# Attention rebuilt: float32 scores of two heads in the two row halves of the array, units of query chunks, a written-out order, 13 weight slots

## The chip, the cores and the metric

One core of one Trainium2 chip. The metric is device microseconds of one execution of the program. The engines go by their names in the profile: PE (TensorE, matrix products), DVE (VectorE), ACT (ScalarE), POOL (GpSimd) and SP (whose queue issues the DMAs).

## What is computed

Causal attention over 2 batches of 12 heads (448 tokens, head dimension 64), its output as 896 tokens by 768, then two feed-forward blocks. The reference, cut:

```python
scores = scale * np.matmul(q, k.transpose(0, 1, 3, 2))      # (2, 12, 448, 448), causal mask
attn = exp(scores - max) / sum
x = np.matmul(attn, v)                                      # -> (896, 768)
h = x @ w_in                                                # 768 x 2048
g = np.where(h >= 1, h, np.where(h <= -1, 0.0, (h + 1) ** 2 / 4))
x = g @ w_out                                               # 2048 x 768
xn = x / sqrt(mean(x * x) + 1e-6) * rms_g
x = (silu(xn @ w_gate) * (xn @ w_val)) @ w_out              # 768 x 1536 twice, 1536 x 768
```

## The kernel before

Activations are held transposed, features on the 128 partitions and 448 tokens (one batch, "half" h) along the free dimension. Every large product is a **three-pass product**: weight and activation are each split into a float32r high part and a low remainder, and three matmuls of 128x448 add up high·high, high·low and low·high. There are 576 such matmuls in the first product (w_in: 16 blocks m, two halves, 6 chunks of contraction), 576 in the second (w_out: 16 chunks kk, two halves), 864 in the gated product and 432 in the last one.

**Weights.** They arrive as 64-bit words, 68 blocks of 128x768. Each block goes through `w_scale` (POOL), `w_sign`, `w_high`, `w_low` (DVE), then `w_hi` (a cast, on POOL for the first blocks and on ACT for the others) and `w_lo` (a subtraction on POOL) into one of the slots; `w_low` also issues the load of the block after next. `w_pace(x)` puts x blocks' worth of these steps into the program at the place where it is called, `w_cap` says how far it may go, and `RATE` holds the values of x. The first MRET = 9 of 13 slots hold w_in blocks while attention runs; the other four are taken up by the split q and k.

**Attention.** One step s of the loop handles one head: `scores` (per head: four bf16 matmuls that write the causal mask into the banks, then eight float32r matmuls, since q and k are split into high and low parts by `split_q` and `split_k` on DVE and POOL; the first pair of heads is `plain`: float32, with the other head's rows of q at zero), `softmax` (per chunk of 112 queries a maximum on DVE and an exponential with its sum on ACT), `transposes` of the head before (ten on PE) and `evac` (three copies on ACT). Once for each pair of heads: `factor` (1/sum: two small DVE operations, a POOL operation, four transposes and a copy on ACT), `pv` (the product with v, both heads at once in the two column halves) and `xsplit` (a DVE product and two POOL operations). Seven PSUM banks go round in one ring for scores, transposes and factor. In the second batch the first 8 blocks of the first product for the first half are laid between as `fill`, in parts of three matmuls, in two banks; `moe_act` finishes each block.

**Order.** Attention is ordered by the Tile scheduler: program order is not the order on the engines there. From the rest of the first product on, `manual_schedule` keeps the written order. Each engine runs its queue strictly in order.

## Time and profile before

| | |
|---|---|
| three runs | 667.75, 669.01, 672.34 us (median 669.01) |
| profiled execution, span | 669.7 us |
| attention (last product with v issued) | 0 to 165.3 us |
| rest of the first product | 165.3 to 257.1 us |
| second product | 257.1 to 405.7 us |
| gated product, from its 37th matmul | 405.7 to 576.8 us |
| last product | 576.8 to 666.1 us |

The span runs from the first to the last instruction of the profiled execution. Busy times of PE include the drain of each matmul, so a busy PE can still take more work.

### The profile page before, as it was taken

The page shows a single profiled execution, that of the slowest core. Times are in us where ns is not written, and L with a number is a line of the kernel's source. Part 1 is how long each engine was busy: PE and PEld are TensorE (multiplying, and loading weights), DVE is VectorE, ACT ScalarE, POOL GpSimd, SP SyncE. Part 2 cuts the span into 40 slices and gives each one's busy share as a digit, 9 for nine tenths or more (in the row PEclk, how much of TensorE's full clock was granted, in tenths as well). Part 3 has the DMA queues.
Part 4 walks back from the last instruction along what each step waited for, and adds up shares of the span by engine and source line. Part 5 has one row for each costly group of instructions (what it writes and reads, how often), then busy time and mean ns, then how long its engine had stood idle before and what let it go on. Part 6 is the DMA issues. An engine that isn't in the chain of part 4 may idle for free.

```text
span 669.7 us, 8507 instructions
## 1 busy us (share of the span) xinstructions
PE 622.5 (93%) x3220; PEld 544.5 (81%) x3220; DVE 494.5 (74%) x634; ACT 211.5 (32%) x488; POOL 278.7 (42%) x215
## 2 busy tenths in 40 slices
PE   4898896899999997799999989999999999999997
PEld 3766674778999996688789978999999999999996
DVE  4999999954598889889544887998887776887100
ACT  2767642453222132222331243122222122422100
POOL 3477787662054343446300440444334434246200
PEclk9998988899999999899999999999999999999999
DMA  8445533220033333333200430324233223255000
GB/s 236 120 117 158 148 113 109 80 90 1 2 139 109 128 103 133 112 125 140 95 0 1 132 104 8 135 94 142 94 98 136 97 95 119 72 179 174 27 32 37
DMA packets 18377, 67.56 MB, mean 101 GB/s; under 512 B 2272, under 2 KB 8288, under 8 KB 18336
## 3 DMA queue, kind: packets, MB, share of 16 engines
q1 hardware_dynamic: 18336, 67.02, 31.3%
q8 instruction: 25, 0.41, 0.2%
q14 instruction: 16, 0.13, 0.1%
HBM read 64.26 MB, written 2.75 MB: 100 GB/s over the span
## 4 chain that ended last, share of the span: by engine, by line
PE 60%; DVE 30%; issue 3%; ACT 3%; DMA 2%; POOL 1%; SPq 0%; ACTq 0%; POOLq 0%; DVEq 0%
PE b L367 30%; PE b L662 13%; PE b L552 10%; DVE af L171 5%; DVE af L159 4%; DVE af L165 4%; DVE af L376 4%; DVE nm L305 3%; DVE ar L507 2%; PE b L351 2%; PE b L288 2%; PE b L334 2%; DVE ar L251 2%; DVE ar L252 2%; DVE ar L260 1%
## 5 line engine op out<-in xcount | busy, mean ns | idle before, releaser
L367 PE MATMUL b<-ar 128*128 128x448 f32 x1440 | 306.4, 371 | 0.0
L367 PEld LDWEIGHTS b<-ar 128*128 128x128 f32 x1440 | 270.1, 189 | 28.0 <-ACT af L341 0.7
L186 POOL TENSOR_TENSOR ar<-af,ar 128x768 fp32r<-128x768 f32 x68 | 127.9, 1881 | 197.2 <-ACT ar L178 196.7
L552 PE MATMUL b<-ar 128*128 128x448 f32 x576 | 124.3, 375 | 14.6 <-DVE ar L507 7.6
L552 PEld LDWEIGHTS b<-ar 128*128 128x128 f32 x576 | 109.7, 192 | 28.9 <-DVE ar L507 10.4
L178 ACT CAST ar<-af 128x768 fp32r<-128x768 f32 x59 | 49.4, 836 | 235.0 <-DVE af L171 235.0
L154 POOL TENSOR_SCALAR af<-af 128x768 f32<-128x768 f32 x68 | 75.2, 1106 | 96.7 <-DMA af<-in_w_out 44.4
L662 PE MATMUL b<-ar 128*128 128x448 f32 x432 | 89.4, 368 | 0.0
L662 PEld LDWEIGHTS b<-ar 128*128 128x128 f32 x432 | 81.1, 188 | 8.2
L171 DVE SCALAR_TENSOR_TENSOR af<-af 128x768 int32<-128x768 int32 x68 | 84.1, 1237 | 1.7
L165 DVE SCALAR_TENSOR_TENSOR af<-af 128x768 int32<-128x768 int32 x68 | 76.7, 1128 | 1.8
L159 DVE TENSOR_SCALAR af<-af 128x768 int32<-128x768 int32 x68 | 61.3, 902 | 12.8 <-POOL af L154 11.4
L309 ACT ACTIVATE af<-b,nm 112x448 f32<-112x448 f32 (+1 forms) x96 | 46.6, 504 | 63.2 <-DVE nm L305 63.0
L507 DVE TENSOR_TENSOR ar<-af,ar 128x448 fp32r<-128x448 f32 x32 | 32.6, 1024 | 27.1 <-ACT ar L506 26.9
L376 DVE SCALAR_TENSOR_TENSOR af<-af 128x448 f32<-128x448 f32 x32 | 32.5, 1016 | 23.4 <-ACT af L375 23.4
L334 PE MATMUL b<-ident,af 112*112 112x112 f32 x240 | 31.3, 277 | 17.1 <-ACT af L309 17.1
L334 PEld LDWEIGHTS b<-ident,af 112*112 112x112 f32 x240 | 26.8, 143 | 21.9 <-ACT af L309 16.0
L261 POOL TENSOR_TENSOR ar<-af,ar 128x448 fp32r<-128x448 f32 x22 | 31.2, 1419 | 23.0 <-DVE ar L260 17.7
L305 DVE TENSOR_REDUCE nm<-b 112x1 f32<-112x448 f32 (+1 forms) x96 | 37.1, 439 | 4.1 <-PE b L288 3.8
L288 PE MATMUL b<-ar 128*112 128x256 f32 (+2 forms) x176 | 35.4, 337 | 0.0
L628 DVE TENSOR_TENSOR af<-af 128x448 f32<-128x448 f32 x24 | 30.5, 1269 | 6.5 <-ACT af L626 5.1
L288 PEld LDWEIGHTS b<-ar 128*112 128x112 f32 x176 | 26.4, 183 | 8.2 <-issue 4.8
(59 smaller groups left out, 452.2 us busy)
## 6 DMA issues: line engine op xcount, KB each, us to landing
af<-in_w_out SPq DMA_DIRECT2D x28, 768.0 KB, 4.2
af<-in_w_in SPq DMA_DIRECT2D x16, 768.0 KB, 4.4
af<-in_w_gate SPq DMA_DIRECT2D x12, 768.0 KB, 4.2
af<-in_w_val SPq DMA_DIRECT2D x12, 768.0 KB, 4.2
af<-in_kT SPq DMA_DIRECT2D x23, 224.0 KB, 3.9
af<-in_v SPq DMA_DIRECT2D x12, 224.0 KB, 3.4
out_T<-af SPq DMA_DIRECT2D x12, 224.0 KB, 1.9
af<-in_qT SPq DMA_DIRECT2D x12, 112.0 KB, 2.4
```

The source lines that it names most:

```text
L154: nc.gpsimd.tensor_scalar(out=c, in0=c, scalar1=2.0 ** -112, scalar2=1.0, op0=ALU.mult, op1=ALU.mult)
L159: nc.vector.tensor_scalar(out=wt[n % 2].bitcast(I32), in0=words(n, 1, I32), scalar1=-2 ** 31, scalar2=0, op0=ALU.bitwise_and, op1=ALU.bitw ...
L165: nc.vector.scalar_tensor_tensor(out=t, in0=words(n, 1, I32), scalar=3, in1=t, op0=ALU.logical_shift_left, op1=ALU.bitwise_or)
L171: nc.vector.scalar_tensor_tensor(out=t, in0=words(n, 0, I32), scalar=29, in1=t, op0=ALU.logical_shift_right, op1=ALU.bitwise_or)
L186: nc.gpsimd.tensor_tensor(out=dst[:, 1, :], in0=wt[n % 2], in1=b32(dst[:, 0, :]), op=ALU.subtract)
L288: nc.tensor.matmul(t[:C, o:o + n], lhsT=qs[i][:, j, c * C:(c + 1) * C], rhs=kk[i][:, j, :n], start=False, stop=(kk is kl), skip_group_chec ...
L305: nc.vector.tensor_reduce(out=nm[:C, c:c + 1], in_=t[:C, o:o + n], axis=AX.X, op=ALU.max, negate=True)
L334: nc.tensor.transpose(t[:C, o + (c - kc) * C:o + (c - kc + 1) * C], pn[:C, poff[c] + kc * C:poff[c] + (kc + 1) * C], ident[:C, :C])
L367: nc.tensor.matmul(out, lhsT=w[:, a, k * P:(k + 1) * P], rhs=x[:, c, k], start=(k == 0 and n == 0), stop=(k == NK - 1 and n == 2))
L376: nc.vector.scalar_tensor_tensor(out=u, in0=u, scalar=1.0, in1=u, op0=ALU.min, op1=ALU.mult)
L552: nc.tensor.matmul(ybs[dm][:, :S], lhsT=w[:, a, dm * P:(dm + 1) * P], rhs=t[:, c], start=(n == 0 and i == 0), stop=(n == NM - 1 and i == 2))
L662: nc.tensor.matmul(ob[:, :S], lhsT=w2[dm][:, kk // NK, a, kk % NK], rhs=x[:, c], start=(kk == 0 and i == 0), stop=(kk == NF - 1 and i == 2))
```

## The change

- **Scores.** q and k are no longer split. Both heads of a pair lie on the 128 partitions (64 each), and each chunk's scores are one float32 matmul per head, with the head's 64 rows only, into a bank of its own. q is scaled in place (POOL, the first pair on DVE).
- **Units.** The loop goes over 36 units n, three for each pair: u = 0 is query chunk 3, u = 1 chunks 2 and 0, u = 2 chunk 1, each for both heads j. Four banks go round for scores, three for transposes and the spread of 1/sum (two once the fill has begun), one for the product with v.
- **Copies after the transposes** are five per pair with a strided output; in the first batch two of them are on DVE. The product with v has ten matmuls instead of eight, with the same number of columns.
- **Order.** The whole body is under `manual_schedule`. Iteration n issues scores(n + 2), every third time the spread and the product with v of the pair before, a part of the fill, transposes(n), maxima and exponentials of unit n + 1 around the copies of unit n, `factor` in the u = 1 iteration, then weight steps and fill.
- **Slots.** All 13 slots hold w_in blocks; w_out takes slots 3 to 12, 0 to 2 and 13 to 15. `w_hi` is on POOL for the first 13 blocks.
- **moe_act**: the square goes to ACT, and one DVE operation with the product's bank as an input remains of two. The fill uses one bank instead of two, and starts at unit 21.

```diff
-    MRET = 9
-    RATE = (0.1, 0.45, 0.65, 0.4, 0.7, 0.8)
+    MRET = 13
+    KK_SLOT = list(range(3, MRET)) + [0, 1, 2, 13, 14, 15]
+    NFILL = 8
+    RATE = (0.15, 0.55, 0.65, 0.55, 0.7, 0.8)
...
+    UNITS = (((3, 0),), ((2, 0), (0, 3 * C)), ((1, 0),))
...
+    def scores(n):
+        g, u = divmod(n, NU)
+        q, k = qraw[g % NQ], kraw[g % NQ]
+        sbank[n] = bs = [turn(sring), turn(sring)]
...
+        at, w = ((3 * C, C), (2 * C, 2 * C), (C, C))[u]
+        for t in bs:
+            nc.tensor.matmul(t[:C, at:at + w], lhsT=identb[:C, :C], rhs=maskb[:C, :w],
+                             start=True, stop=False, skip_group_check=True)
+        for c, o in UNITS[u]:
+            for j in range(2):
+                r = slice(D * j, D * (j + 1))
+                nc.tensor.matmul(bs[j][:C, o:o + (c + 1) * C], lhsT=q[r, c * C:(c + 1) * C], rhs=k[r, :(c + 1) * C],
                                  start=False, stop=True, skip_group_check=True)
...
         nc.scalar.activation(u, ps, ACTF.Relu, bias=half, scale=0.5)
-        nc.vector.scalar_tensor_tensor(out=u, in0=u, scalar=1.0, in1=u, op0=ALU.min, op1=ALU.mult)
-        nc.vector.tensor_tensor(out=G[h][:, m], in0=u, in1=ps, op=ALU.max)
+        nc.scalar.activation(u, u, ACTF.Square)
+        nc.vector.scalar_tensor_tensor(out=G[h][:, m], in0=u, scalar=1.0, in1=ps, op0=ALU.min, op1=ALU.max)
...
-    hbanks = deque([6, 7])
+    hbanks = deque([6])
...
+    for n in range(last):
+        g, u = divmod(n, NU)
+        if n == NP * NU + 3:
+            for m in range(NFILL):
                 push_in(m, 0)
+            tring.remove(6)
+            left[0] = 2 * (last - n)
+        if n + 2 < NN:
+            scores(n + 2)
+        if u == 0 and g:
+            spread()
+            pv(g - 1)
+            load_v(g + 1)
         fillin()
+        if n < NN:
+            transposes(n)
+        more = n + 1 < NN
+        if more:
+            maxima(n + 1, 0)
+            exps(n + 1, 0)
+        if n < NN:
+            evac(n, 0, nc.scalar)
+        if more:
+            maxima(n + 1, 1)
+            exps(n + 1, 1)
+        if n < NN and u < 2:
+            evac(n, 1, nc.vector if g < NP else nc.scalar)
+        if (n + 1) % NU == NU - 1 and more:
+            factor((n + 1) // NU)
+        if u == 0:
+            if g:
+                xsplit(g - 1)
+        elif u == 1:
+            scale_q(g + 2, nc.gpsimd)
+        else:
+            load_qk(g + 3)
         flush()
+        w_pace(RATE[0] if n < NP * NU else RATE[1])
         fillin()
...
-                w_cap[0] = MRET + m + 1 if m < 6 else NM + min(4 + m - 6, NM)
+                w_cap[0] = MRET + m + 1
```

**ACT in the first batch, before** (one head: four exponentials, L309, the three copies of the head before, L340 to L342, and the next head's first exponential; b_ are PSUM banks):

```order
L309 ACTIVATE af,sums<-b_275,nm 112x448
L309 ACTIVATE af,sums<-b_276,nm 112x336
L309 ACTIVATE af,sums<-b_277,nm 112x224
L309 ACTIVATE af,sums<-b_277,nm 112x112
L340 COPY af<-b_300 112x448
L341 COPY af<-b_301 112x336
L342 COPY af<-b_302 112x336
L309 ACTIVATE af,sums<-b_331,nm 112x448
```

The same place **after** (from a u = 2 iteration into the u = 0 iteration: L268 exponentials, L301 copies after transposes, L318 the copy of the spread factors):

```order
L268 ACTIVATE af,sums<-b_244,nm 112x448
L301 COPY af<-b_281 112x2x2x112
L268 ACTIVATE af,sums<-b_245,nm 112x448
L318 COPY af<-b_301 128x448
L268 ACTIVATE af,sums<-b_273,nm 112x336
L268 ACTIVATE af,sums<-b_273,nm 112x112
L301 COPY af<-b_319 112x4x112
L268 ACTIVATE af,sums<-b_274,nm 112x336
L268 ACTIVATE af,sums<-b_274,nm 112x112
```

Between the exponentials of the two heads of every unit there now stands a copy that waits for the transposes of the unit before.

**DVE in the first batch, before** (L251 and L252 split q, L260 casts k, L316 and L317 are `factor`, L171 a weight step, L305 maxima):

```order
L252 SCALAR_TENSOR_TENSOR ar<-af,ar 64x448
L260 CAST ar<-af 128x448
L251 TENSOR_SCALAR ar<-af 64x448
L260 CAST ar<-af 128x448
L252 SCALAR_TENSOR_TENSOR ar<-af,ar 64x448
L316 TENSOR_SCALAR rs<-sums 112x8
L171 SCALAR_TENSOR_TENSOR af<-af 128x768
L305 TENSOR_REDUCE nm<-b_399 112x1
L305 TENSOR_REDUCE nm<-b_400 112x1
```

The same engine **after** (L260 maxima, L303 a copy after transposes, L335 `xsplit`, L309 and L310 `factor`, L151 a weight step):

```order
L335 TENSOR_TENSOR af<-b_307,af 128x448
L260 TENSOR_REDUCE nm<-b_295 112x1
L260 TENSOR_REDUCE nm<-b_296 112x1
L303 COPY af<-b_353 112x4x112
L309 TENSOR_SCALAR rs<-sums 112x8
L310 RECIPROCAL rs<-rs 112x8
L260 TENSOR_REDUCE nm<-b_344 112x1
L260 TENSOR_REDUCE nm<-b_345 112x1
L151 TENSOR_SCALAR af<-af 128x768
```

The five q and k operations are gone; the maxima of the next pair's first unit (b_344, b_345) stand right behind `factor`, which needs the last exponential of the pair.

**DVE in the first product, before** (L159, L165, L171 are the three weight steps, L376 and L377 `moe_act`):

```order
L165 SCALAR_TENSOR_TENSOR af<-af 128x768
L171 SCALAR_TENSOR_TENSOR af<-af 128x768
L376 SCALAR_TENSOR_TENSOR af<-af 128x448
L377 TENSOR_TENSOR af<-af,b_2095 128x448
L159 TENSOR_SCALAR af<-af 128x768
L165 SCALAR_TENSOR_TENSOR af<-af 128x768
L171 SCALAR_TENSOR_TENSOR af<-af 128x768
L376 SCALAR_TENSOR_TENSOR af<-af 128x448
L377 TENSOR_TENSOR af<-af,b_2122 128x448
```

and **after** (L151, L157, L163 the weight steps, L354 what remains of `moe_act`):

```order
L157 SCALAR_TENSOR_TENSOR af<-af 128x768
L163 SCALAR_TENSOR_TENSOR af<-af 128x768
L354 SCALAR_TENSOR_TENSOR af<-af,b_1990 128x448
L151 TENSOR_SCALAR af<-af 128x768
L157 SCALAR_TENSOR_TENSOR af<-af 128x768
L354 SCALAR_TENSOR_TENSOR af<-af,b_2017 128x448
L163 SCALAR_TENSOR_TENSOR af<-af 128x768
L354 SCALAR_TENSOR_TENSOR af<-af,b_2043 128x448
```

One DVE operation per block and half is gone, and the weight steps keep their rate.

## Rows read from the trace of the kernel before

**Rows 1.** The page: the span.

```profile
span 669.7 us, 8507 instructions
```

**Rows 2.** Busy time of each engine in two stretches (start:end us, length, then busy us and count of PE, its weight loads, DVE, ACT and POOL, granted clock, DMA share, GB/s): attention in the first batch, and the rest of the first product after attention.

```profile
0.00:77.00 77.00, 62.13 (x420) 47.29 (x421) 65.39 (x129) 45.87 (x158) 45.53 (x51) 0.93 0.55 149
...
165.30:257.10 91.80, 91.80 (x446) 83.40 (x446) 74.28 (x82) 22.00 (x34) 34.73 (x24) 1.00 0.28 95
```

**Rows 3.** The longest wait between 10 and 165 us (who waited for whom: us in total, times, longest).

```profile
ACT af L309 <- DVE nm L305: 63.0, 21, 8.8
```

**Rows 4.** Instruction groups of DVE up to 165.3 us, shapes apart (line, engine, operation, names, shapes, count | busy us, mean ns | idle before): the split of q, the cast of k, a maximum, and the first operation of `factor`.

```profile
L251 DVE TENSOR_SCALAR ar<-af 64x448 fp32r<-64x448 f32 x22 | 17.0, 771 | 3.5 <-DMA af<-in_qT 3.2
L252 DVE SCALAR_TENSOR_TENSOR ar<-af,ar 64x448 fp32r<-64x448 f32 x22 | 15.0, 681 | 0.7
L305 DVE TENSOR_REDUCE nm<-b 112x1 f32<-112x448 f32 x24 | 14.8, 617 | 3.6 <-PE b L288 3.4
L260 DVE CAST ar<-af 128x448 fp32r<-128x448 f32 x22 | 13.4, 615 | 0.4
L316 DVE TENSOR_SCALAR rs<-sums 112x8 f32<-112x8 f32 x12 | 9.4, 782 | 2.3 <-ACT af L309 2.1
```

**Rows 5.** Timeline of PE (start us, us, instructions): the first matmuls of the product with v of pairs 0, 5 and 11.

```profile
24.12 0.59 PE L351 MATMUL b<-af 112*64 112x448 f32 x2
...
74.86 0.60 PE L351 MATMUL b<-af 112*64 112x448 f32 x2
...
163.20 0.60 PE L351 MATMUL b<-af 112*64 112x448 f32 x2
```

**Rows 6.** Busy time of the three-pass products (L367) up to 165.3 us (PE, then the weight loads).

```profile
0.00:165.30 165.30, 35.32 (x133) 24.74 (x133) 0.94 0.41 119
```

**Rows 7.** The chain that ended last (start us, us, what): ten transposes in a row; the cast of a weight block at the same point of six neighbouring cycles in the first product, the first and the last of them; the first operation of the RMS norm behind the second product's first half; the last product.

```profile
40.25 0.96 PE b L334 x10
...
183.09 0.84 ACT ar L178
...
249.18 0.84 ACT ar L178
...
333.55 0.63 ACT ar L567
...
576.85 89.29 PE b L662 x432
```

**Rows 8.** Instruction groups of DVE over the whole span, shapes apart: the three weight steps, the two operations of `moe_act`, and an operation of the RMS norm that reads a bank as the one that remains in `moe_act` does.

```profile
L171 DVE SCALAR_TENSOR_TENSOR af<-af 128x768 int32<-128x768 int32 x68 | 84.1, 1237 | 1.7
L165 DVE SCALAR_TENSOR_TENSOR af<-af 128x768 int32<-128x768 int32 x68 | 76.7, 1128 | 1.8
L159 DVE TENSOR_SCALAR af<-af 128x768 int32<-128x768 int32 x68 | 61.3, 902 | 12.8 <-POOL af L154 11.4 <-ACT af L665 1.4
L376 DVE SCALAR_TENSOR_TENSOR af<-af 128x448 f32<-128x448 f32 x32 | 32.5, 1016 | 23.4 <-ACT af L375 23.4
L377 DVE TENSOR_TENSOR af<-af,b 128x448 f32<-128x448 f32 x32 | 19.8, 618 | 0.9
L569 DVE SCALAR_TENSOR_TENSOR ar<-b,gvec,ar 128x448 fp32r<-128x448 f32 x12 | 8.2, 679 | 1.8 <-ACT af L568 1.8
```

**Rows 9.** Timeline of PE: the spread of 1/sum (L322), the product with v of both heads (L351) and the masks of the next scores (L278).

```profile
43.84 0.60 PE L322 MATMUL b<-ident,af 112*128 112x112 f32 x4
44.38 2.11 PE L351 MATMUL b<-af 112*64 112x448 f32 x16
46.41 0.41 PE L278 MATMUL b<-maskb,identb 112*112 112x112 bf16 x4
```

**Rows 10.** Timeline of ACT: exponentials of one head (L309) and the copies behind them (L340 and L341); then the first PE instruction that waited for the exponential at 51.17; then a copy on ACT (L323) and the four PE transposes that it waited for.

```profile
51.17 0.63 ACT L309 ACTIVATE af<-b,nm 112x448 f32<-112x448 f32 x1 [4.28 <-DVE nm L305]
51.80 0.53 ACT L309 ACTIVATE af<-b,nm 112x336 f32<-112x336 f32 x1
52.31 0.45 ACT L309 ACTIVATE af<-b,nm 112x224 f32<-112x224 f32 x1
52.73 0.36 ACT L309 ACTIVATE af<-b,nm 112x112 f32<-112x112 f32 x1
53.06 0.54 ACT L340 COPY af<-b 112x448 f32<-112x448 f32 x1
53.47 0.47 ACT L341 COPY af<-b 112x336 f32<-112x336 f32 x1
...
51.95 0.21 PE L278 MATMUL b<-maskb,identb 112*112 112x112 bf16 x1 [2.62 <-ACT af L309]
...
36.79 0.60 PE L322 MATMUL b<-ident,af 112*128 112x112 f32 x4
37.48 0.53 ACT L323 COPY af<-b 128x448 f32<-128x448 f32 x1 [0.92 <-PE b L322]
```

**Rows 11.** Timeline of PE at the start: the float32 scores of heads 0 and 1 (L284, four chunks each).

```profile
4.85 4.00 PE L284 MATMUL b<-af 128*112 128x448 f32 x8 [1.64 <-DMA af<-in_kT]
8.89 2.10 PE L284 MATMUL b<-af 128*112 128x448 f32 x8
```

**Rows 12.** Busy time of PE in two neighbouring stretches of the first batch (busy us and count, granted clock, DMA share, GB/s).

```profile
47.80:51.20 3.40, 1.53 (x15) 1.00 0.16 32
51.20:54.60 3.40, 2.65 (x12) 0.77 0.88 234
```

More of the change, by code (lines that the diff above doesn't have):

```diff
@@ new lines, with transposes @@
+    tbank = {}
+    def transposes(n):
+        u = n % NU
+        if u < 2:
+            tbank[n] = bs = [turn(tring), turn(tring)]
+        else:
+            t = turn(tring)
+            tbank[n] = bs = [t[:, :2 * C], t[:, 2 * C:4 * C]]
+        for j in range(2):
+            o = 0
+            for c, _ in UNITS[u]:
+                for kc in range(c + 1):
+                    nc.tensor.transpose(bs[j][:C, o:o + C], Pn[:C, j, poff[c] + kc * C:poff[c] + (kc + 1) * C],
+                                        ident[:C, :C])
+                    o += C
+        if u == 2:
+            tbank[n] = [t]
@@ new lines, in evac @@
+    def evac(n, i, eng):
+        u = n % NU
+        t = tbank[n][i]
+        if u == 2:
+            out = PT[:C, :, 1:5:3, :]
+            src = t[:C, :4 * C].rearrange("p (j k d) -> p j k d", j=2, k=2)
+        else:
+            first = 3 if u == 0 else 2
+            out = PT[:C, i, first:first + 10:3, :]
+            src = t[:C, :4 * C].rearrange("p (k d) -> p k d", k=4)
+        if eng is nc.scalar:
+            nc.scalar.copy(out, src)
+        else:
+            eng.tensor_copy(out, src)
@@ L492 @@
     flush()
-    with tc.manual_schedule():
-        seq = [(MRET - 1, 0)] + [(m, 1) for m in range(MRET)]
-        for m in range(MRET, NM):
+    if True:
+        seq = [(m, 1) for m in range(NFILL)]
+        for m in range(NFILL, NM):
             seq += [(m, 0), (m, 1)]
```

246 lines of the change are left out of this document (79 added, 167 removed).

## The prediction

> **What bounds the kernel now.** I read the span and the busy time by stage first [rows 1, 2], then the waits, then one stage at a time. The reader should see three different stages. Everything after attention is a dense stream of three-pass matmuls: the last product runs 432 of them in 89.29 us, 0.2067 us each [rows 7], and 2,448 of them (576 + 576 + 864 + 432) are 506.0 us of the 669.7.
>
> In attention DVE is the engine that the others wait for: it is busy 65.39 us of the first 77 [rows 2], and ACT's exponentials waited 63.0 us for its maxima [rows 3]. The splits of q and k alone are 17.0 + 15.0 + 13.4 = 45.4 us of DVE [rows 4]. A pair takes (74.86 - 24.12) / 5 = 10.15 us in the first batch and (163.20 - 74.86) / 6 = 14.7 us in the second, where fill and weight steps are laid between [rows 5].
>
> Up to 165.3 us 133 three-pass matmuls have run [rows 6]. The other 2,315 are 478.5 us, and behind the last one, at 576.85 + 89.29 = 666.1, 3.6 us are left. So 669.7 - 165.3 - 478.5 - 3.6 = 22.3 us are holes in PE's stream. The first half of the second product, from 257.1 to 333.55 [rows 7], needs 288 x 0.2067 = 59.5 us and takes 76.4: 16.9 of the 22.3 lie there, and 5.4 in its second half and the norms.
>
> Those 16.9 are DVE's delay from the first product. There the cast of a weight block comes back on the chain every (249.18 - 183.09) / 5 = 13.2 us [rows 7]. Two weight blocks are 2 x (0.90 + 1.13 + 1.24) = 6.5 us of DVE [rows 8]; at 0.65 blocks a product they go with 3.08 products, whose `moe_act` is 3.08 x (1.02 + 0.62) = 5.0. The remaining 1.6 us fit a wait for ACT's cast and Relu. PE needs only 3.08 x 18 x 0.2067 = 11.5 us for 3.08 products, so DVE falls back 1.7 us in each of about seven cycles, some 12 us in all, and the second product, which wants its activation split by DVE, pays.
>
> **The change part by part.** *Attention, first batch.* The splits go, and DVE no longer sets the pace: of its own work a pair keeps 3 us of maxima and some 4 us more. What sets it is the written order. PE's masks for unit n + 2 wait for the last exponential of unit n; then come the scores, at u = 0 also spread and product with v, then the transposes of unit n; ACT copies the first head's and only then does the second head's exponentials of unit n + 1, for which PE waits again. Per round, from rows: a mask 0.1; spread until product with v 0.54 and that product 2.03 [rows 9]; four transposes until ACT's copy starts 0.69; that copy 0.41; the last exponential until PE goes on 51.95 - 51.17 = 0.78 for 448 columns, which is 0.15 over the distance to the next (0.63), so 0.51 + 0.33 + 0.15 = 0.99 for 336 and 112 and 0.42 + 0.15 = 0.57 for 224 [rows 10].
>
> The scores have no row in this form. A whole head in float32 took 2.10 us with the drain [rows 11], 1.87 at four passes of 1,120 columns and 2.4 GHz. The nearest row for two heads at once is the product with v in two column halves: also 1,120 columns for each head, and 2.03 us for both [rows 9], so halves ran side by side there. I take the same for row halves: 0.78 us for 448 columns (or 336 + 112), 0.40 for 224. The upper bound is one after the other, twice that.
>
> Rounds: u = 0 is 0.1 + 0.40 + 0.54 + 2.03 + 0.69 + 0.41 + 0.99 = 5.2; u = 1 is 0.1 + 0.78 + 0.69 + 0.41 + 0.57 = 2.6; u = 2 is 0.1 + 0.78 + 0.69 + 0.41 + 0.78 = 2.8. That is 10.5 us a pair. `factor` adds to it: DVE waits there for the last exponential of the pair, with the maxima of the next pair queued behind. Factor's two small operations are 0.17 to 0.78 [rows 4] and about 0.2 (I take 0.5 together, as POOL, which competes, has little to do now), half a weight step 0.5, the maximum 0.6, the exponential 0.63: 2.3 us, where the copy could have gone at 1.6. So 11.2 us a pair, 1 us more than now: DVE's 45 us turn into hand-overs.
>
> *Second batch.* 0.55 blocks a unit are 1.8 us of DVE in place of 0.5, again behind `factor`: 12.5 us for pair 6. From unit 21 on 144 matmuls, 29.8 us, go into 34 places, 0.88 each; one place lies in PE's part of each round, which shows at u = 0 and u = 1 and hides behind DVE at u = 2: 14.3. The 1.4 blocks that end in each pair put a Relu, a square and a DVE operation (0.68, as L569 [rows 8]) ahead of maxima and exponentials: by the same rows 1.6 us late when it happens before the transposes, 0.4 behind them, so 1.4 a pair, and some 0.2 for the single fill bank: 15.9.
>
> *Start and end.* k and q of the first pair come with two transfers in place of three, where PE waited until 4.85 for the third [rows 11]; then 448 columns at half clock (1.5), a maximum, two exponentials: the first round begins at about 8.3 us. The last product with v and the remaining fill add 2.6. Attention: 8.3 + 6 x 11.2 + 12.5 + 5 x 15.9 + 2.6 = 170.1 us, 4.8 later than now, but with 11 more matmuls done: 2,304 remain, 476.2 us.
>
> *First and second product.* `moe_act` on DVE falls from 1.63 to 0.68 us. A cycle of two blocks is then 6.5 + 3.08 x 0.68 = 8.6 us and a wait of 1 to 2.9 us (cast, Relu and square in a row on ACT), at most 11.5, PE's own time: DVE no longer falls back. The 32 squares cost ACT about 18 us, beside 22.0 busy of 91.8 [rows 2]. By rate, 13 + 20 x 0.65 + 4 x 0.55 = 28.2 blocks are ready at the second product against 9 + 20 x 0.65 + 4 x 0.4 = 23.6 before, so DVE has fewer to do in it. Of the 16.9 us I leave 3 for the first chunks; the 5.4 stay, as the norms and the second half's pacing are untouched. Holes: 8.4; bounds 5.4 and 22.3.
>
> POOL loses its 22 subtractions for k and takes 11 scalings of q, and SP issues fewer transfers; neither is waited for on this path, and the weight steps on POOL fit beside the longer rounds.
>
> Sum: 170.1 + 476.2 + 8.4 + 3.6 = 658.3 against 669.7. The median of the runs is 669.0, 0.1% under the profiled span, so **658 us**, 1.7% faster; 1% is about what a measurement here tells from no change.
>
> **The rivals.** *The hand-overs are all there is* (DVE never late, `moe_act` hidden): 10.5, 10.5 and 10.5 + 3 x 0.88 = 13.1 us a pair, attention 8.3 + 63 + 10.5 + 65.5 + 2.6 = 149.9, holes 5.4: 635 us. For it: DVE has 7 to 8 us of work in an 11 us pair. Against: in-order queues with `factor` in front of the maxima.
>
> *The clock falls in the first batch* (slower). PE was busy 1.53 of 3.4 us before a stretch whose granted clock was 0.77 [rows 12], part of it at 1.2 GHz. With hand-overs in every round PE streams only some 6 of 11.2 us. At 1.2 GHz PE's parts (3.5, 1.2 and 1.2 us, of the last 0.6 hidden) double: 5.2 us a pair, 31 over six, 690 us. It decides from four of the six pairs on, 679. Against: 11 us of rounds hold 3.5 us in one piece.
>
> *The row halves run one after the other:* 0.37 + 0.75 a pair and 0.15 to 0.75 at u = 2, 1.3 to 1.9 us, twelve times: 673 to 681.
>
> *Changing the tile shape costs.* Spread until product with v took 0.54, with four transposes at 0.096 [rows 7, 9]: up to 0.16 us where the shape changes. The new scores add six such changes a pair, two of them hidden: 0.6 to 1.0 us, twelve times, 666 to 670. The Trainium skill, TensorEngine Tiling (Array Packing), Key Properties, speaks against the change here: changing the tiling mode drains the engine, while tiles of one mode work independently; it gives no price. The trace agrees with the second half by the product with v; for the first, the 0.16 us is all that it could hide.
>
> *Nothing comes of slots and* `moe_act`: holes stay 22.3, 672 us.
>
> **How the numbers follow.** Forecast 0.45 (648 to 668; 0.37 faster, 0.08 same), hand-overs alone 0.18 (faster), clock 0.15 (0.13 slower, 0.02 same), halves in turn 0.10 (half same, half slower), tile shape 0.08 (same), holes stay 0.04 (same). Faster 0.55, same 0.27, slower 0.18. The range, 634 to 683, leaves out about the fastest and slowest tenth.
>
> **What would show it.** Pairs 11.2 us apart in the first batch and 16 in the second, PE idle before masks on exponentials, ACT on transposes; score matmuls of two heads starting together; attention's end at 170; no hole over 1 us in the first half of the second product; DVE with idle time in the first product. It is wrong if pairs come 10 or 13 us apart, if the clock row shows long stretches at half, or if score matmuls of a unit follow each other.

## The result, and the profile after

The changed kernel takes 678.95 us (four runs, 676.09 to 681.26), the kernel before 670.67 beside it: ratio 1.013, 95% interval 1.009 to 1.018. That is 1.3% slower, where 1.7% faster was forecast (658 us; the time lies in the range 634 to 683). Profiled execution after, the page's span, busy times, granted clock in 40 slices, chain by engine, and two groups:

```profile
span 678.4 us, 8418 instructions
...
PE 625.6 (92%) x3244; PEld 536.2 (79%) x3244; DVE 417.5 (62%) x547; ACT 226.1 (33%) x492; POOL 259.9 (38%) x207
...
PEclk9788989977899999999999998999999999999999
...
PE 83%; DVE 7%; ACT 7%; issue 2%; DMA 0%; ACTq 0%; SPq 0%
...
L344 PE MATMUL b<-ar 128*128 128x448 f32 x1440 | 303.8, 370 | 11.8 <-DVE af L354 11.8
...
L249 PE MATMUL b<-maskb,identb 112*112 112x112 bf16 (+1 forms) x72 | 16.0, 238 | 31.1 <-ACT af L268 29.0
```

The same row of the clock, before:

```profile
PEclk9998988899999999899999999999999999999999
```

PE waited 29.0 us for exponentials ahead of masks (L249), 11.8 us for the DVE operation that empties the one fill bank (L344), and the clock row has more slices at 7 and 8 in attention. Stretches of the kernel after, columns as in [rows 2]: attention to its last product with v; the first batch from the start of its first round; pairs 7 to 10; the two halves of the second product; two single rounds u = 0 (of pairs 2 and 3); then attention cut at the product with v of pair 5.

```profile
0.00:193.70 193.70, 149.12 (x918) 98.61 (x918) 97.91 (x188) 88.08 (x267) 91.19 (x93) 0.89 0.31 100
...
8.57:82.46 73.89, 55.54 (x377) 34.20 (x376) 36.69 (x89) 36.40 (x120) 27.52 (x31) 0.91 0.29 96
98.58:176.51 77.93, 64.86 (x366) 45.02 (x366) 42.13 (x73) 33.67 (x99) 41.78 (x35) 0.86 0.30 100
286.04:346.81 60.77, 59.27 (x289) 53.93 (x288) 30.04 (x32) 15.60 (x26) 15.15 (x11) 1.00 0.20 66
346.81:410.90 64.09, 61.78 (x290) 55.29 (x289) 40.48 (x50) 18.95 (x33) 13.27 (x9) 0.97 0.16 51
...
32.76:38.19 5.43, 4.31 (x38) 2.87 (x38) 1.57 (x5) 2.81 (x11) 0.00 (x0) 1.00 0.64 198
44.01:51.12 7.11, 6.00 (x38) 3.62 (x38) 1.52 (x5) 2.81 (x11) 1.11 (x2) 0.76 0.14 36
...
8.57:84.30 75.73, 57.33 (x387) 35.14 (x385) 36.69 (x89) 36.40 (x120) 27.52 (x31) 0.90 0.28 94
84.30:191.80 107.50, 85.68 (x501) 60.15 (x500) 57.77 (x96) 47.65 (x141) 60.03 (x51) 0.86 0.28 91
```

And of the kernel before, its second product's first half:

```profile
257.09:332.88 75.79, 64.00 (x290) 55.92 (x288) 61.71 (x60) 21.86 (x35) 37.14 (x24) 0.95 0.38 125
```

**Where the time went.** The last matmul with v starts at 193.7 us instead of 165.1, with 126 fill matmuls done instead of 132: 28.6 + 6 x 0.2067 = 29.8 us lost. The first half of the second product takes 60.8 us in place of 75.8: 15.0 won. Together that would be 14.8 slower; the spans differ by 8.7. The other 6 us are the dense stream: the last product's 432 matmuls, from the chain after, took 87.57 us in place of 89.29 [rows 7], 0.2027 us each, and the first product went at the same pace. The traces of the experiments have either pace in kernels of both families (below).

```profile
587.24 87.57 PE b L653 x432
```

**The two equal rounds** show the clock's price. Both have the same 38 matmuls. In one the clock was 1.00 and it took 5.43 us; in the other it was 0.76, that is 2 x 0.24 x 7.11 = 3.4 us at 1.2 GHz, and it took 7.11: 1.7 longer, half of the slow time. PE was busy through all of the 3.4 us. The Trainium skill, TensorE: Matmul & The Clock Gate, "HAM oscillation", counts the same half as lost; the trace agrees here. By the clock's records attention has 44.4 us at half clock, where before it had 20.5. (The profiled executions of after_warm and before_rows, below, were among the slower ones of their kernels, so of these two executions only the attention is compared.)

### The profile page after: what moved, and what is told of

It is laid out like the page before. It is cut to its first block, busy times and chain, and to the rows that moved or that the text cites. A ratio compares the mean times of both kernels' runs of the same rounds, so it can differ in the third digit from the quotient of the medians.

```text
span 678.4 us, 8418 instructions
## 1 busy us (share of the span) xinstructions
PE 625.6 (92%) x3244; PEld 536.2 (79%) x3244; DVE 417.5 (62%) x547; ACT 226.1 (33%) x492; POOL 259.9 (38%) x207
## 4 chain that ended last, share of the span: by engine, by line
PE 83%; DVE 7%; ACT 7%; issue 2%; DMA 0%; ACTq 0%; SPq 0%
PE b L344 42%; PE b L543 14%; PE b L653 13%; PE b L329 5%; PE b L254 4%; ACT af L268 4%; PE b L284 2%; DVE af L157 2%; DVE af L163 1%; ACT af L301 1%; DVE ar L498 1%; PE b L317 1%; PE b L249 1%; DVE nm L260 1%; DVE af L354 1%
## 5 line engine op out<-in xcount | busy, mean ns | idle before, releaser
L344 PE MATMUL b<-ar 128*128 128x448 f32 x1440 | 303.8, 370 | 11.8 <-DVE af L354 11.8
L344 PEld LDWEIGHTS b<-ar 128*128 128x128 f32 x1440 | 270.1, 189 | 39.6 <-DVE af L354 13.8
L543 PE MATMUL b<-ar 128*128 128x448 f32 x576 | 121.2, 371 | 3.8 <-DVE ar L498 3.4
L146 POOL TENSOR_SCALAR af<-af 128x768 f32<-128x768 f32 x68 | 73.2, 1077 | 93.4 <-DMA af<-in_w_out 44.4
L163 DVE SCALAR_TENSOR_TENSOR af<-af 128x768 int32<-128x768 int32 x68 | 87.7, 1290 | 1.8
L653 PE MATMUL b<-ar 128*128 128x448 f32 x432 | 87.7, 365 | 0.0
L157 DVE SCALAR_TENSOR_TENSOR af<-af 128x768 int32<-128x768 int32 x68 | 78.4, 1153 | 1.8
L151 DVE TENSOR_SCALAR af<-af 128x768 int32<-128x768 int32 x68 | 53.5, 787 | 8.4 <-POOL af L146 8.4
L268 ACT ACTIVATE af<-b,nm 112x336 f32<-112x336 f32 (+2 forms) x96 | 47.4, 499 | 31.5 <-DVE nm L260 31.3
L354 DVE SCALAR_TENSOR_TENSOR af<-af,b 128x448 f32<-128x448 f32 x32 | 19.8, 619 | 40.9 <-ACT af L353 40.8
L249 PE MATMUL b<-maskb,identb 112*112 112x112 bf16 (+1 forms) x72 | 16.0, 238 | 31.1 <-ACT af L268 29.0
L254 PEld LDWEIGHTS b<-af 64*112 64x112 f32 x192 | 16.0, 193 | 36.0 <-issue 27.3
L301 ACT COPY af<-b 112x448 f32<-112x448 f32 x48 | 25.6, 533 | 45.4 <-PE b L284 44.9
L254 PE MATMUL b<-af 64*112 64x448 f32 (+3 forms) x192 | 37.0, 488 | 2.5 <-DVE af L228 2.5
L260 DVE TENSOR_REDUCE nm<-b 112x1 f32<-112x336 f32 (+2 forms) x96 | 36.8, 436 | 3.1 <-PE b L254 3.1
L497 ACT CAST ar<-af 128x448 fp32r<-128x448 f32 x32 | 18.0, 565 | 56.6 <-PE b L543 56.5
```

The costliest lines, as they stand in the source:

```text
L146: nc.gpsimd.tensor_scalar(out=c, in0=c, scalar1=2.0 ** -112, scalar2=1.0, op0=ALU.mult, op1=ALU.mult)
L151: nc.vector.tensor_scalar(out=wt[n % 2].bitcast(I32), in0=words(n, 1, I32), scalar1=-2 ** 31, scalar2=0, op0=ALU.bitwise_and, op1=ALU.bitw ...
L157: nc.vector.scalar_tensor_tensor(out=t, in0=words(n, 1, I32), scalar=3, in1=t, op0=ALU.logical_shift_left, op1=ALU.bitwise_or)
L163: nc.vector.scalar_tensor_tensor(out=t, in0=words(n, 0, I32), scalar=29, in1=t, op0=ALU.logical_shift_right, op1=ALU.bitwise_or)
L254: nc.tensor.matmul(bs[j][:C, o:o + (c + 1) * C], lhsT=q[r, c * C:(c + 1) * C], rhs=k[r, :(c + 1) * C], start=False, stop=True, skip_group_ ...
L260: nc.vector.tensor_reduce(out=stat[g][0][:C, j, c:c + 1], in_=sbank[n][j][:C, o:o + (c + 1) * C], axis=AX.X, op=ALU.max, negate=True)
```

## The experiments

All times are medians of four to ten runs, but of two for after_nofill, after_nofill_slow, after_late, after_early, after_half_early and after_oldmoe; the ratio is against the kernel before run beside it. The end of attention (last product with v) and the half-clock time in it come from each kernel's profiled execution.

| kernel | us | ratio, 95% | attention ends | at half clock |
|---|---|---|---|---|
| before | 668 to 671 | | 165.1 | 20.5 |
| after | 678.95 | 1.013 (1.009 to 1.018) | 193.7 | 44.4 |
| after_warm | 675.8 | 1.008 (1.004 to 1.012) | 187.2 | 20.5 |
| after_wfirst | 677.8 | 1.015 (1.010 to 1.021) | 192.6 | 34.1 |
| after_nofill | 689.2 | 1.030 (1.023 to 1.037) | 175.5 | 51.1 |
| after_nofill_slow | 682.3 | 1.020 (1.013 to 1.027) | 159.8 | 32.4 |
| after_bare_warm | 665.2 (one run) | | 149.4 | 5.8 |
| after_late | 693.2 | 1.036 (1.027 to 1.045) | 201.9 | 47.8 |
| after_early | 697.3 | 1.044 (1.041 to 1.047) | 210.8 | 68.3 |
| after_place | 677.8 | 1.016 (1.009 to 1.022) | 192.0 | 44.4 |
| after_sched | **656.6** | 0.981 (0.976 to 0.986) | 173.0 | 20.5 |
| after_half | 672.1 | 1.004 (1.000 to 1.007) | 183.2 | 34.1 |
| after_half_warm | 670.7 | 1.002 (0.997 to 1.006) | 181.1 | 23.9 |
| after_half_early | 682.2 | 1.021 (1.018 to 1.024) | 195.0 | 51.2 |
| after_half_place | 667.3 | 0.998 (0.994 to 1.002) | 182.3 | 37.5 |
| after_oldmoe | 704.8 | 1.054 (1.044 to 1.063) | 195.0 | 41.0 |
| before_square | **655.1** | 0.981 (0.976 to 0.987) | 165.4 | 13.7 |
| before_rows | 668.0 | 0.996 (0.992 to 1.000) | 177.6 | 23.9 |
| before_square_k | 664.7 | 0.993 (0.990 to 0.997) | 173.5 | 27.3 |
| before_pad | 669.8 | 1.003 (0.999 to 1.006) | 166.4 | 20.5 |

### The clock

**after_warm**

```diff
+        for _ in range(6):     # in scores(n), ahead of the masks
+            nc.tensor.matmul(bs[0][:C, :2 * C], lhsT=identb[:C, :C], rhs=maskb[:C, :2 * C],
+                             start=True, stop=False, skip_group_check=True)
```

> The changed kernel with six more mask matmuls (224 columns, bf16) ahead of each unit's first mask, into a bank that the mask overwrites; they run while PE would wait for the last exponential. If the half-clock stretches (44 us of attention in the changed kernel) cost half their length, as the rounds say (7.11 against 5.42 us with 3.41 us at half clock), the first batch's pairs come 11.2 us apart throughout, the half-clock stretches in attention all but vanish, and the time falls by 15 to 22 us. If the clock is not the cause, the time stays or rises by what the added matmuls delay (36 units x 0.1 to 0.5 us).

Its first batch (same columns):

```profile
8.57:77.26 68.69, 60.52 (x495) 42.61 (x492) 36.75 (x89) 36.33 (x119) 27.52 (x30) 1.00 0.31 103
```

With PE busy 60.5 of 68.7 us instead of 55.5 of 73.9 the clock stays at 1.00, and the same work is done 5.2 us earlier, in spite of more matmuls (495 against 377). So in the first batch the clock is a cause, not a companion. But attention as a whole gains only 6.5 us, and the time did not fall by the 15 to 22 expected, with the half clock down by 24: in the second batch the extra matmuls cost time of their own. Pair 8 has the clock at 1.00 throughout in after and takes 15.4 us; with them it takes 17.2, with 1.2 us at half clock.

**after_bare_warm** (after_nofill_slow, below, with the same six matmuls)

> after_nofill_slow (no fill, 0.15 blocks of weight steps a unit) with the six extra bf16 mask matmuls of after_warm in each unit: the bare hand-overs of attention, with PE kept busier while it would be short of work. In after_nofill_slow attention ended at 159.8 us with 32.4 us of it at half clock. If a half-clock stretch costs half its length there and nothing else disturbs, attention ends at 159.8 - 16.2 = 143.6 when no stretch is left, 143 to 147, and pairs take 11.2 to 11.9 throughout. If the long u = 0 rounds have another cause that only goes along with the clock, attention ends above 152.

```profile
90.00:135.00 45.00, 38.95 (x328) 27.31 (x324) 19.87 (x50) 27.23 (x88) 17.19 (x19) 1.00 0.22 68
```

Pairs of 11.2 to 11.9 us in both batches at clock 1.00. Attention ends at 149.4, 2.4 us above the range; 10.4 of the 16.2 us came.

### The weight steps

**after_wfirst** (u = 1 iteration: weight steps ahead of `factor`, so that they no longer wait for the pair's last exponential)

> The changed kernel with the weight steps of each u = 1 iteration issued ahead of factor instead of behind it, so that DVE does them while it would wait for the pair's last exponential. If the weight steps behind factor hold up the next pair's maxima (u = 2 rounds of 6.3 to 8.3 us in the second batch against 3.0 in the first), those rounds fall by 1.5 to 2.5 us, six of them, and the time by 8 to 14 us. If the clock alone makes the second batch long, the change is under 3 us.

Attention ends 1.1 us earlier, under the 3 us expected if the clock alone makes the second batch long. The first batch is 4.4 us longer, and the second wins that back. Its pair 10 had no half clock, where the same pair in after had 9.5 us of it (after first; from the second mask of a pair to that of the next):

```profile
155.46:176.56 21.10, 18.39 (x93) 12.57 (x93) 11.49 (x22) 8.07 (x24) 8.74 (x7) 0.78 0.21 68
```

```profile
158.51:175.24 16.73, 14.02 (x94) 10.18 (x93) 9.54 (x19) 8.07 (x24) 7.32 (x6) 1.00 0.25 68
```

The same 27 fill matmuls are in both, and 4.4 us lie between them, 46% of the slow time. The weight steps are not the reason: after_early, below, with DVE busy 8.2 us in its pair 10, takes 21.1 us at a clock of 0.77.

**after_early**

```diff
-    RATE = (0.15, 0.55, 0.65, 0.55, 0.7, 0.8)
+    RATE = (0.45, 0.3, 0.65, 0.55, 0.7, 0.8)
```

> The kernel after with 0.45 and 0.3 blocks of weight steps a unit in the two batches, in place of 0.15 and 0.55; the same 13 blocks, the same place at the end of each iteration. If the place is the trouble (behind the factor, ahead of the next maxima), the first batch gets longer by 6 to 12 us (pair 6, at 0.55, was 2 us longer than the first batch's pairs apart from the clock) and the second shorter by as little as 5: attention ends at 193 to 202, time 677 to 687. If only the number beside the fill counts: first batch within 3 us, the second 10 us or more shorter, attention 180 to 187, time 663 to 672.

Its pairs 7 to 10:

```profile
115.29:193.64 78.35, 65.81 (x366) 46.21 (x366) 28.62 (x63) 33.58 (x98) 26.90 (x27) 0.85 0.21 65
```

DVE does 28.6 us of work in them instead of 42.1, and they take 78.35 us instead of 77.93: pair by pair 19.3, 15.4, 22.6 and 21.1 against 18.9, 15.4, 22.6 and 21.1. So the weight steps have no part in the length of these four pairs. In the first batch they cost much more than expected: pairs of 14.3 to 17.6 us with 3.4 to 9.1 us of half clock each. Both ranges of the expectation were missed (attention 210.8, time 697.3).

**after_place** (weight steps only at the end of u = 2 iterations, rates 0.4 and 0.4)

```diff
-        w_pace(RATE[0] if n < NP * NU else RATE[1])
+        if u == 2 or n >= NN:
+            w_pace(3 * (RATE[0] if n < NP * NU else RATE[1]))
```

> The kernel after, written order throughout, with the weight steps only once for each pair, at the end of the u = 2 iteration (in front of the round with spread and product with v, the longest on PE, where DVE has least to do), 0.4 blocks a unit in both batches. If the place decides: first batch 78 to 87 us with 7 blocks done, attention ends at 176 to 188, time 660 to 672. If not: as after_early's first theory, time 677 to 687.

The first batch ends at 84.9 us with six weight blocks done: the place does matter there (100.4 in after_early; 82.5 in after, with two blocks). Pairs 7 to 10 take 16.7, 15.4, 22.6 and 21.1: the last three as in after, and the time is the same. The expected 660 to 672 missed. Pair 7 had the clock at 1.00 here and 4.9 us at half clock in after (after first):

```profile
98.63:117.49 18.86, 15.80 (x90) 10.63 (x90) 8.18 (x17) 8.26 (x24) 11.06 (x9) 0.87 0.37 130
```

```profile
99.17:115.84 16.67, 13.59 (x91) 9.61 (x90) 8.18 (x17) 8.25 (x24) 6.69 (x8) 1.00 0.27 89
```

With practically the same instructions on PE, DVE and ACT the difference is 2.2 us, 45% of the slow time. Pair 9 gives less: 21.5 us in after_wfirst with 3.4 at half clock, 22.6 in after with 7.6. Pair 8, at 1.00 in after, after_wfirst, after_early and after_place, takes 15.4 us in all four. So in the second batch too the half clock costs time, with the fill in place: nearly half of its length in pairs 7 and 10, a quarter in pair 9. Why it falls in a pair of one kernel and not in the same pair of another is not shown.

### The fill

**after_nofill** and **after_nofill_slow** (no part of the first product in attention; in the second also 0.15 for 0.55 in `RATE`)

```diff
-            for m in range(NFILL):
-                push_in(m, 0)
-            tring.remove(6)
-            left[0] = 2 * (last - n)
+            pass
...
-        seq = [(m, 1) for m in range(NFILL)]
-        for m in range(NFILL, NM):
+        seq = []
+        for m in range(NM):
```

> The kernel after without any of the first product inside attention: all 576 of its matmuls come behind attention (with 0.65 blocks of weight steps a product for 28 of the 32). Compared inside attention: in the kernel after, pairs 7 to 10 took 18.9, 15.4, 22.6 and 21.1 us and attention ended at 193.7 with 126 of these matmuls done. Theory A (a block of the fill that ends puts its Relu, square and DVE operation in front of the next maxima and exponentials, and its one bank makes PE wait): pairs 6 to 11 fall to 12 to 13.5 us, attention ends at 158 to 166, and the time is 666 to 674, since the 126 matmuls (25.8 us) come back behind it. Theory B (the weight steps behind the factor, in front of the next maxima, are what is long): pairs stay at 16 us or more, attention ends above 178, time 688 or more.

> As after_nofill, and the second batch has the first batch's rate of weight steps (0.15 blocks a unit in place of 0.55), so that nothing but attention is left in it. If fill and weight steps together are the whole cause: pairs 6 to 11 take 11.2 us as in the first batch (more by half of each stretch at half clock), attention ends at 150 to 156, and the time is 658 to 668 (7.2 blocks fewer are ready at its end, which the first product has to make up). If something else of the second batch is long (copies all on ACT, POOL, the clock): pairs stay above 13 us. Against after_nofill it prices the weight steps: theory B expects 4 us a pair or more between the two, theory A 1 to 2.

Pairs 7 to 10 of the first:

```profile
99.00:157.30 58.30, 41.32 (x264) 24.93 (x264) 37.78 (x64) 27.81 (x88) 39.78 (x34) 0.84 0.39 130
```

and of the second:

```profile
93.99:143.70 49.71, 36.74 (x264) 22.91 (x264) 19.87 (x50) 27.47 (x88) 18.59 (x20) 0.93 0.19 61
```

The four pairs take 77.9 us with fill, 58.3 without, 49.7 without fill and with few weight steps; the first batch's pace would be 45. So the fill is 19.6 / 4 = 4.9 us a pair, nearly all of the time of its 25.5 matmuls (102 in the four pairs; 25.5 x 0.2067 = 5.3). With half of the slow time taken off either side (22.0 and 18.6 us) it is 4.5: little of it is hidden. The weight steps are 2.1 a pair without fill, of which the clock takes (2 x 0.16 x 58.3 - 2 x 0.07 x 49.7) / 2 / 4 = 1.5. With nothing between, rounds are those of the first batch (11.25 us, plus half of each slow stretch). after_nofill's attention, 175.5, lies between what theories A and B gave; its 689.2 us is in B's range, and the 2.1 us a pair for the weight steps are nearer to A's 1 to 2. after_nofill_slow missed: attention 159.8 for 150 to 156, time 682.3 for 658 to 668.

**after_late** (Relu, square and DVE operation of an ended block at the end of the iteration; the next block begins in a later place)

> The kernel after with the Relu, square and DVE operation of a fill block that has ended moved to the end of the iteration, behind the next unit's exponentials and the copies; the next block begins in a later place, so nothing waits in a circle. Same work. Theory A: 1.5 to 3 us less for each of the seven or eight blocks that end in attention, attention ends 10 to 20 us earlier (174 to 184), time 660 to 669. Theory B: less than 4 us changes.

The contrary: 8 us later, outside both theories. The place where they stand in after looks bad in its timeline (a block's last part L344, its three operations, the maxima behind them, the next part that waited for the bank, the exponential that waited for the maximum):

```profile
136.15 0.88 PE L344 MATMUL b<-ar 128*128 128x448 f32 x3
...
137.06 0.64 ACT L352 ACTIVATE af<-b,half 128x448 f32<-128x448 f32 x1 [2.26 <-PE b L344]
137.73 0.58 ACT L353 ACTIVATE af<-af 128x448 f32<-128x448 f32 x1
138.33 0.62 DVE L354 SCALAR_TENSOR_TENSOR af<-af,b 128x448 f32<-128x448 f32 x1 [3.20 <-ACT af L353]
138.87 1.27 DVE L260 TENSOR_REDUCE nm<-b 112x1 f32<-112x336 f32 x4
...
139.01 0.88 PE L344 MATMUL b<-ar 128*128 128x448 f32 x3 [1.22 <-DVE af L354]
...
139.59 0.54 ACT L268 ACTIVATE af<-b,nm 112x336 f32<-112x336 f32 x1 [1.29 <-DVE nm L260]
```

But with one bank a later end also holds back the next block: PE's waits for that bank from 82 us to the end of attention are 22.2 us in after_late (us in total, times, longest) and 11.8 in after.

```profile
PE b L344 <- DVE af L354: 22.2, 7, 5.3
```

What a better place would give is not shown.

### The written order

**after_sched** (the written order begins behind attention; before that the scheduler orders the same statements)

> The kernel after with the written order of attention taken back: the same statements, units, banks and rates, but the scheduler orders them as in the kernel before; the written order begins behind attention. If the written hand-overs (one engine at a time, weight steps and a block's end ahead of maxima) are what costs, attention ends at 165 to 182 and the time is 650 to 668. If the units and the four score banks themselves allow no more, attention ends at 188 to 200 and the time is 673 to 686. If the scheduler puts the weight steps early, in front of the maxima, as it did in before_rows (24.7 us of ACT's waits on maxima from 25 to 75 us), the first batch gets longer than 73.9 us, by 5 to 15 us, and the second shorter.

Cut at the product with v of pair 5:

```profile
8.00:85.70 77.70, 64.93 (x388) 39.42 (x384) 60.60 (x110) 36.13 (x124) 56.54 (x51) 0.94 0.47 156
85.70:171.10 85.40, 78.04 (x505) 56.88 (x504) 40.83 (x78) 44.97 (x138) 37.91 (x36) 0.94 0.23 76
```

This part alone is 22.3 us: 656.6, and attention ends 20.7 earlier. Up to pair 5 the scheduler is no quicker (77.7 us against 75.7), but DVE does 60.6 us of work there instead of 36.7: 8 weight blocks are done by then instead of 2. Behind it 85.4 us against 107.5, with PE busy 78.0 of the 85.4. The clock is part of that: behind pair 5 the written order has 29.4 us at half clock and the scheduler's 10.4, and half of the difference, an estimate, would be 9.5 of the 22.1 us.

**after_half** and **after_half_warm** (written order in the first batch, scheduler's in the second; the other with the six extra matmuls in the first batch)

> The kernel after, with the written order in the first batch only (to unit 17) and the scheduler's order for the rest of attention. Whole written order: attention ends at 193.7, the first batch at 82.5 us; scheduler's order in all of attention: 173.0, and its second batch takes some 74 us. If the second batch is where the written order loses: first batch unchanged (80 to 84), the rest 74 to 86 us, attention ends at 157 to 169, time 642 to 656. If what the scheduler wins comes from work pulled across the batches (weight steps early), attention ends at 172 to 188, time 657 to 672.

> after_half with the six extra bf16 mask matmuls in each unit of the first batch alone. In after_warm they took the half clock out of the first batch and ended it at 77.3 instead of 82.5 us. If that time is kept by what follows: attention 4 to 6 us earlier than in after_half, the time as much less. If the second batch gives it back (weights or the clock): within 2 us of after_half.

after_half, the same cut:

```profile
8.57:84.00 75.43, 54.55 (x381) 33.75 (x379) 40.19 (x93) 37.04 (x122) 30.48 (x33) 0.91 0.30 104
84.00:181.30 97.30, 81.28 (x508) 58.62 (x507) 54.51 (x94) 45.04 (x139) 56.81 (x53) 0.89 0.33 108
```

Half of the gain: 107.5 becomes 97.3, not 85.4. That the written order loses in the second batch alone falls. The held clock brought 2.1 us, not 4 to 6.

**after_half_early** and **after_half_place** (0.45 and 0.3 blocks; the other as after_half_warm, with the first batch's steps at the end of u = 2 iterations only)

> after_half (written order in the first batch, scheduler's in the second) with 0.45 and 0.3 blocks a unit: 8 blocks in the first batch as the scheduler has there. Number beside the fill: from the end of the first batch the rest takes 84 to 88 us in place of 99, and attention ends at 165 to 175 if the first batch keeps within 3 us, 171 to 182 if the place makes it 6 to 10 us longer. If the rest stays at 97 or more, the number of blocks isn't it.

> after_half_warm (written first batch with the clock held, scheduler's second batch) with 0.45 blocks a unit in the first batch, put at the end of the u = 2 iterations only, and 0.3 in the second. All three causes together (clock in the first batch, place, number beside the fill): first batch 77 to 83, the rest 84 to 88, attention 162 to 171, time 644 to 656. If the rest stays near 99: attention 176 or more, time 660 or more.

From pair 5 to pair 11 after_half_early takes 92.9 us and after_half_place (87.7 to 180.4) 92.7, not 84 to 88: with fewer weight steps beside the fill 4.4 of the 11.9 us go, and 4.1 us of half clock with them, so the steps' own part is not shown apart from the clock's. In them pair 5 comes later, at 100.3 and 87.7 us. Why the scheduler's order of the whole is 7 us better still in its second part was not settled; it has 6.0 us less at half clock there, half of which would be 3.0.

### Single parts

**before_square** and **after_oldmoe** (the `moe_act` of the change in the kernel before, and the old one in the kernel after)

```diff
-        nc.vector.scalar_tensor_tensor(out=u, in0=u, scalar=1.0, in1=u, op0=ALU.min, op1=ALU.mult)
-        nc.vector.tensor_tensor(out=G[h][:, m], in0=u, in1=ps, op=ALU.max)
+        nc.scalar.activation(u, u, ACTF.Square)
+        nc.vector.scalar_tensor_tensor(out=G[h][:, m], in0=u, scalar=1.0, in1=ps, op0=ALU.min, op1=ALU.max)
```

> The kernel before with one part of the change alone: the square of moe_act on ACT, one DVE operation instead of two. If DVE's delay in the first product makes the holes of the second, as the forecast has it, the holes (22 to 24 us) fall to 8 to 12 and the time by 10 to 16 us. If the four more slots or the faster rate are what closes them, the time falls by less than 5 us.

> The kernel after with one part undone: the square back on DVE, two DVE operations with the bank as an input of the second, as before. If the holes of the second product hang on this part alone, as before_square shows from the other side, its first half takes 70 to 77 us in place of 60.8, attention changes by less than 4 us, and the time is 685 to 693. If the 13 slots are the better half of it, less than 4 us change.

The second product's first half, before_square:

```profile
257.39:321.73 64.34, 60.52 (x290) 53.45 (x288) 50.35 (x48) 19.43 (x31) 31.64 (x20) 1.00 0.37 123
```

after_oldmoe:

```profile
288.08:368.74 80.66, 66.68 (x290) 58.55 (x289) 43.27 (x49) 18.29 (x30) 22.71 (x16) 0.87 0.21 74
```

75.8 becomes 64.3 by this part alone; 60.8 becomes 80.7 without it. (after_oldmoe's time, 704.8, and the 80.7 lie above the expected 685 to 693 and 70 to 77.) The holes behind attention, counted as what starts of neighbouring dense matmuls over 0.25 us apart have beyond the pitch, fall from 24 to 11 us with it and rise from 9 to 27 without. It is the whole gain of the change, 12.6 us, and the 13 slots add at most the 3.5 between 64.3 and 60.8.

**before_rows** (before_square, with float32 scores of 64 rows for each head, no splits, the scheduler's order)

> The kernel before, in its scheduler's order with its seven banks and its weight slots, with two parts of the change alone: the square on ACT (as in before_square, 655.1 us) and the float32 scores with 64 rows for each head, no splits of q and k (one scaling for each pair). One head after the other, so nothing of units or of a written order. If the splits on DVE are what attention waits for and the hand-overs of the written order are what the changed kernel loses: pairs of the first batch 8.5 to 9.5 us (10.15 before), attention ends at 150 to 160, time 643 to 651. If float32 scores one head after the other (2.1 us against 1.1) make PE the bound, or PE falls to half clock more: no gain, 653 to 662.

From the product with v of pair 5 to that of pair 10 (before_rows, then before_square):

```profile
97.10:166.60 69.50, 69.50 (x428) 52.03 (x427) 24.63 (x62) 41.21 (x131) 13.21 (x18) 1.00 0.12 37
```

```profile
77.20:154.40 77.20, 65.09 (x426) 51.23 (x425) 64.94 (x104) 40.60 (x132) 56.76 (x44) 0.96 0.33 105
```

12.9 us slower than before_square, outside both expected ranges, with attention 12.2 later. In this stretch before_rows is 7.7 us the faster: PE has no gap left, and DVE is at 24.6 of 69.5. The loss lies ahead of it: pair 5 comes at 97.1 us instead of 77.2, with nine weight blocks done by then instead of two and 23.9 us at half clock instead of 6.8; half of that difference, an estimate, would be 8.5 of the 19.9. The scheduler has moved the weight steps too, so this run doesn't price the float32 scores, nor DVE's 45 us, by themselves.

**before_square_k** (k's rounding copy on ACT)

> before_square (655.1 us) and one more DVE operation on ACT: the rounding copy of k in the split (0.62 us, once for each head from the second pair on, 22 of them). DVE is busy 63.5 of the first 77 us of attention and ACT 43.4. If DVE sets the pace there, attention gets shorter by most of 22 x 0.62 = 13.6 us: 643 to 650. If ACT's queue (exponentials, copies) is as tight as DVE's, no change, 651 to 659.

Neither: 9.6 us slower than before_square, attention 8.2 later. DVE was not short of time in a way that this move helps; the scheduler's order changes with it, so no single wait can be named.

**before_pad** (the kernel before with the arrays behind the mask moved by 224 bytes, as in after)

> The kernel before with the mask tile twice as wide and nothing else: both work arenas move up by 224 bytes, to where the changed kernel has them. If the place of the operands is why the dense matmuls come 0.2027 us apart in the changed kernel and 0.2066 in the kernel before, the pitch in the gated and last product falls to 0.2027 and the time by 5 to 9 us. If it is the chip or the run, nothing changes.

No difference in time, though in this trace the pitch did fall. Its last product (from the chain) beside that of after_nofill_slow, a kernel with after's addresses:

```profile
574.27 87.57 PE b L662 x432
```

```profile
588.83 89.29 PE b L650 x432
```

0.2027 and 0.2067 us a matmul. before_square, at the addresses of before, took 87.57 us, where before took 89.29. Moved addresses are not what sets it.

## Why the prediction was wrong, point by point

**Right: the hand-overs, as a sum.** The first round starts at 8.57 us (8.3). Undisturbed rounds are 5.42, 2.79 and 3.03, 11.25 us a pair (11.2). But the 0.7 set aside for `factor` lies as 0.2 on each of the three rounds (5.2, 2.6, 2.8), so the split of the sum is not borne out. The row halves run side by side (timeline of PE: mask, the scores of one unit with 336 and 112 columns for each head, and the transpose behind them):

```profile
41.03 0.26 PE L249 MATMUL b<-maskb,identb 112*112 112x224 bf16 x1 [0.64 <-ACT af L268]
41.22 1.02 PE L254 MATMUL b<-af 64*112 64x336 f32 x8
42.16 0.31 PE L284 MATMUL b<-ident,af 112*112 112x112 f32 x1
```

From the first score to the next transpose are 0.94 us (0.78 was taken, and twice that for one after the other). So the halves in turn are out. The 0.16 above 0.78 could be the change of tile shape, which would be up to 0.6 a pair; then the sum was right in part by luck, since it had nothing for that and 0.7 for `factor`. The Trainium skill's drain at a change of mode (TensorEngine Tiling (Array Packing), Key Properties) is neither shown nor excluded by that.

**Right: `moe_act` and the holes.** 8.9 us of holes between the matmuls behind attention and 1.0 ahead of the first of them (8.4), mainly by that part, shown from both sides.

**Wrong: attention, 170.1.** With all 144 fill matmuls it is 193.7 + 18 x 0.2067 = 197.4. By the terms of the sum: start +0.3; 6 x 11.2 became 73.9, +6.7; pair 6, 12.5 became 16.1, +3.6; four of the pairs at 15.9 became 77.9, +14.3; the last pair and the end, 18.5, became 20.9, +2.4. The step that failed is that the sum was made at full clock. Of the 27.3 some 19 are the clock's. Measured are 5.2 in the first batch (after_warm) and, against the same pairs with less of the half clock, 2.2, 1.1 and 4.4 in pairs 7, 9 and 10 (after_place and, for the last two, after_wfirst). Half of the slow time, an estimate, is 2.7 in pair 6, 1.7 for the 3.4 us at half clock that pair 9 kept in after_wfirst, and 1.7 in the last pair. The clock stood as a rival, but in the first batch only and as a whole batch at 1.2 GHz (5.2 us a pair, chance 0.15). What came were single stretches, most of them in the second batch, for which the forecast had no price at all.

**Mis-sized: the fill.** It was to add 3.4 us a pair: 1.8 for the two of its six places that were to show, and 1.6 for the blocks that end. The kernels with and without fill differ by 4.9, 4.5 apart from the clock. Pairs of the second batch that ran at full clock took 16.7 (pair 7), 15.4 (pair 8) and 16.7 us (pair 10), and pair 9 took 21.5 with 3.4 us at half clock, against 15.9. Pair 6, with half of its slow time taken off, is 13.4 (12.5).

**Not foreseen: the pitch.** 2,304 matmuls at 0.2028 instead of 0.2067 gave 9 us back in this execution, so the profiled execution flatters the change: 27.3 lost in attention and 1.5 in holes, less 9, are the 20 between 678.4 and 658.3.

**The change as a whole.** It is three things: `moe_act` (-12.6 us), the written order of attention (+22.3), and the rest (units, row halves and slots as one sum: 656.6 against before_square's 655.1, nothing clear of noise; none of them was run singly). Both before_square and after_sched beat both kernels.

## What to carry to other kernels

Matmuls that are put into a chain of hand-overs by hand counted almost in full here (4.5 to 4.9 of 5.3 us a pair). The same statements left to a scheduler were 22 us faster, with PE busy for a larger share and less half clock; which of its moves does it is not shown. Where PE is to wait in every round, price the half clock (here nearly half of the slow time in most places, a quarter in pair 9) in the sum itself, and test it by adding idle matmuls or by the same rounds in runs where the clock held. A change of several parts is best run part by part first: here one line held the gain.

## What the runs showed of the hardware

The clock fell, at 45.5 us for one, in rounds in which PE waited no longer than 1.1 us at a time (timeline of PE after, the mask of the round that lost 1.7 us; then the 3.4 us that followed, columns as in [rows 2]):

```profile
44.06 0.21 PE L249 MATMUL b<-maskb,identb 112*112 112x112 bf16 x1 [1.07 <-ACT af L268]
...
45.47:48.88 3.41, 3.41 (x20) 1.84 (x18) 0.00 (x0) 1.40 (x5) 0.00 (x0) 0.50 0.02 5
```

PE was busy 55.5 us of the 73.9 of the first batch, and more matmuls without use made the same rounds shorter: 68.7 us. Half clock need not cost time everywhere: before and before_square end attention at 165.1 and 165.4 us with 20.5 and 13.7 us of it. The dense stream has two paces at a granted clock of 1.00. The last product's 432 matmuls of 448 columns took 87.56 or 87.57 us in 15 of the 20 traces and 89.29 in the other five, 0.2027 and 0.2067 us each and nothing between. The pace can also change between the products of one run: before's second product went partly at 0.203. Neither the addresses nor any part of the change goes along with it; its cause stays open.
